# A decode attention block on one core: loop bodies of one group instead of two, a second buffer for the first chunk of transposed K, and the MLP's vector work behind the fourth tile

## The chip, the cores and the metric

The kernel runs on one core of one Trainium2 chip. TensorE (PE in the profile) multiplies matrices, with its weight loads shown as PEld; VectorE (DVE), ScalarE (ACT) and GpSimd (POOL) do the rest, and SyncE (SP) issues nearly all DMA transfers. The metric is the device time of one execution in microseconds (us). Lower is better.

## The reference

One token of a decoder block for two sequences (B = 2), with a cache of 32768 keys per head. Everything is float32.

```python
xn = _layernorm(x)                      # x: 2 x 1 x 512
q = (xn @ wq)                           # 32 query heads of 128
scores = q . k_cache * 128**-0.5        # 8 KV heads, 32768 keys, each serves 4 query heads
p = softmax(scores)
s = (p . v_cache) @ wo                  # 32 heads of 128 -> 512
gate, up = xn @ W_gate, xn @ W_up       # 512 -> 1792 each
g = silu((gate * (gate > 0) * up) @ W_down)
return x + s * g
```

K and V are 2 x 8 x 32768 x 128 floats each, 537 MB together. The weights come to 28 MB. All of it is read once.

## The kernel before

**Tiles and steps.** A group is one pair of sequence b and KV head hk. There are 16 groups (`NG`), and `group(g)` walks b fastest. A tile is 8192 keys of a group (`TK`): 4 MB of K and 4 MB of V. A group has four tiles (`NU`), so there are 64 (`NK`). The program goes in steps s = 0 to 68. Step s transposes K tile s and computes its scores; the softmax weights and V of tile s - 4 follow in the same step, so that a group's maximum is known before its weights are used.

**One step on the engines.** VectorE transposes the K tile in four chunks (`k_transpose(t, c)`, L645) from one of two K buffers (`kslot`) into one buffer per chunk (`kts[c]`). TensorE multiplies each chunk with the group's query (`scores`, L656): 16 matmuls of 512 columns, in four column strips. VectorE takes the scores of the tile before out of PSUM, with a running maximum (`take_scores`, L672). In each fourth step VectorE, TensorE and ScalarE form the group's maximum and the exponentials (`tile_maximum`, `maximum`), and the outcome of the group that is complete is scaled and turned (`take_o`, `finish_group`). TensorE brings the weights into their layout (`weights`), VectorE transposes them (`take_weights`), and in odd steps TensorE multiplies the weights of two tiles with V (`values`).

**Transfers.** V comes as 8 MB for two tiles (`load_vv`) into one buffer `wide`, which has no twin: the next pair can be asked for only when `values` has read the last one. SP takes its list in order and waits in front of each transfer until its buffer is free. The list begins: wq, K0, K1, W_gate and W_up, K2, K3, W_down, K4, K5, V0/1 (the first 8 MB of V), K6, K7, V2/3, and then two K and one V for each two steps. wq, W_gate, W_up, W_down all pass through `wide` before V does; V0/1 waits for the MLP's last product, which reads W_down there. K tile t + 2 waits for the fourth transposition of tile t.

**The MLP.** `mlp_gu` (step 1) multiplies with W_gate and W_up. `mlp_vector` (L590, five VectorE instructions) forms the hidden row, and `mlp_down` (L620, 56 matmuls of 128 columns) multiplies it with W_down. Both stand in the list `taken` of step 3: behind the first of tile 3's four transpositions and in front of `take_scores`.

**Waits and loops.** `Program.op` records every operation with the buffers that it reads and writes, and derives from them what each engine waits for. The order on each engine is that of the calls. `Program.emit` writes the list of each engine out; on VectorE and TensorE the steps from 8 to 63 become a loop whose body is `PERIOD` = 8 steps (two groups), seven rounds. Two groups are needed in a body because many buffers alternate by group (`st`, `mx`, `ls`, `os_`, `ops`, `qcur` and others have two sets), and because `finish_group` does its vector part only for the second sequence of a pair. TensorE's program holds 335 matmuls ahead of the loop, 272 in its body and 121 behind it, 728 in all.

**The first chunk.** `kts[0]` is one buffer, as are the other three: the first transposition of a tile waits until TensorE has read the first chunk of the tile before to the end.

Of the kernel before, what the change touches and what calls it, by code (L numbers as in the profile page):

```python
# [8 lines left out]
P = 128  # L9
Q = 32  # L10
# [6 lines left out]
PERIOD = 8  # L17
# [144 lines left out]
def decode_block_kernel(nc, x, kc, vc, wq, wo, wg, wu, wd, out):  # L162
# [14 lines left out]
    NST = 2 * NU  # L177
# [11 lines left out]
    kts = [sbuf(f"kts{c}", P, NR * P, align=ALIGN) for c in range(NC)]  # L189
    st = [sbuf(f"st{i}", P, NR * Q) for i in range(NST)]  # L190
# [16 lines left out]
    qcur = [sbuf(f"qcur{b}", P, 4, Q) for b in range(B)]  # L207
    ots = sbuf("ots", P, HKV, 4, 32)
    heads = sbuf("heads", P, B, REP, 32)
    fold = sbuf("fold", P, 32)  # L210
    stat = sbuf("stat", 32, 8)
    mx = [sbuf(f"mx{i}", P, NU) for i in range(2)]
    ls = [sbuf(f"ls{i}", P, NU) for i in range(2)]
    mcol = [sbuf(f"m{i}", P, 1) for i in range(2)]
    mr = [sbuf(f"mr{i}", 1, REP) for i in range(2)]
    nb = [sbuf(f"nb{i}", P, 1) for i in range(2)]
    lcol = [sbuf(f"l{i}", P, 1) for i in range(2)]
    rl = [sbuf(f"rl{i}", P, 1) for i in range(2)]
# [5 lines left out]
    ops = [bank(f"o{i}") for i in range(2)]  # L224
    ps_m = [bank(f"m_ps{i}") for i in range(2)]

# [69 lines left out]
    for i in range(2):  # L296
        dve(lambda e, i=i: e.memset(ops[i], 0.0), w=[f"o{i}"])
# [48 lines left out]
    for b in range(B):  # L346
        dve(lambda e, b=b: e.tensor_copy(heads[:, b, :, b], head), ["head"], ["heads"])
# [26 lines left out]
    xt = st[4].rearrange("p (r m) -> p r m", m=Q)  # L374
# [18 lines left out]
        ["st4"],  # L393
# [78 lines left out]
    def project_q():  # L472
        pq = ps_m
        for half in range(2):
            pe(
                chain(
                    [
                        mm(
                            pq[half][32 * c : 32 * c + 32, :],
                            xn[:, k, :],  # L480
                            wqt[:, k, half, c * 512 : (c + 1) * 512],
                            k == 0,
                            k == NKC - 1,
                        )
                        for k in range(NKC)
                        for c in range(4)
                    ]
                ),
                ["st4", "wide"],
                [f"m{half}"],  # L490
            )
# [52 lines left out]
        for g in range(2):  # L544
            take_query(g)

    def take_query(g):
        b, hk = group(g)
        pg.op(
            "POOL" if g >= 2 else "DVE",  # L550
            lambda e: e.tensor_copy(qcur[b], qt[:, b, hk]),
            ["qt"],
            [f"qcur{b}"],
        )
# [15 lines left out]
    def mlp_gu(which, i):  # L570
# [15 lines left out]
            ["st4", "wide", f"wide_{which}"],  # L586
# [3 lines left out]
    def mlp_vector():  # L590
        g, u = os_
        for i in range(2):
# [11 lines left out]
                st[NST - 1][:, : FI * Q], g[:, :FC].rearrange("p (f i) -> p i f", i=FI)  # L604
            ),
            ["os0"],
            [f"st{NST - 1}"],
# [12 lines left out]
    def mlp_down():  # L620
        ht = st[NST - 1][:, : FI * Q].rearrange("p (i m) -> p i m", m=Q)
        pe(
            chain(
                [
                    mm(
                        ps_m[0][32 * c : 32 * c + 32, :P],
                        ht[:, i, :],
                        wdt[:, i, c * P : (c + 1) * P],
                        i == 0,
                        i == FI - 1,  # L630
                    )
                    for i in range(FI)
                    for c in range(4)
                ]
            ),
            [f"st{NST - 1}", "wide"],
            ["m0"],
        )
        act(
            lambda e: e.activation(gy, ps_m[0][:, :P], AF.Silu, bias=zero, scale=1.0),  # L640
            ["m0", "zero"],
            ["gy"],
        )

    def k_transpose(t, c):  # L645
        src = kslot[t % 2]
        dve(
            lambda e: e.transpose(  # L648
                kts[c].rearrange("p (h n) -> p h n", h=2),
# [3 lines left out]
            [f"kts{c}"],  # L653
        )

    def scores(t):  # L656
        b, _ = group(t // NU)
        ps = ps_s[t % 2]

        def one(e, c):  # L660
            part = kts[c].rearrange("p (r e k) -> p r e k", e=4, k=Q)
            return mm(
                ps[Q * c : Q * c + Q, :], qcur[b][:, e, :], part[:, :, e, :], e == 0, e == 3
            )

        for c in range(NC):
            pe(one(0, c), [f"kts{c}", f"qcur{b}"], [f"s{t % 2}"])
        pe(chain([one(e, c) for e in (1, 2) for c in range(NC)]), [f"qcur{b}"], [f"s{t % 2}"])
        for c in range(NC):
            pe(one(3, c), [f"kts{c}", f"qcur{b}"], [f"s{t % 2}"])  # L670

    def take_scores(t):  # L672
        g, u = divmod(t, NU)
        dve(
            lambda e: e.tensor_scalar(  # L675
                st[t % NST],
# [5 lines left out]
                accum_out=mx[g % 2][:, u : u + 1],  # L682
            ),
            [f"s{t % 2}"],
            [f"st{t % NST}", f"mx{g % 2}_{u}"],
        )

    def tile_maximum(g):
        i = g % 2
        dve(  # L690
            lambda e: e.reduce_max(mcol[i], mx[i], axis=AX.X),  # L691
            [f"mx{i}_{u}" for u in range(NU)],
            [f"mcol{i}"],
        )
        pe(
            lambda e: e.transpose(ps_m[0][:1, :P], mcol[i], ident),  # L696
            [f"mcol{i}", "ident"],
            ["m0"],
        )

    def maximum(g):
        i = g % 2
# [3 lines left out]
                mr[i],  # L706
# [5 lines left out]
            [f"mr{i}"],  # L712
# [3 lines left out]
                mrow[:, :, :4, :], mr[i].unsqueeze(1).unsqueeze(1).to_broadcast([1, 4, 4, REP])  # L716
            ),
            [f"mr{i}"],
# [7 lines left out]
        dve(lambda e: e.tensor_copy(nb[i], pr[:, 256:257]), ["m0"], [f"nb{i}"])  # L726
        for u in range(NU):
            t = (g * NU + u) % NST
            act(
                lambda e, t=t, u=u: e.activation(  # L730
                    st[t], st[t], AF.Exp, bias=nb[i], scale=1.0, accum_out=ls[i][:, u : u + 1]
                ),
                [f"st{t}", f"nb{i}"],
                [f"st{t}", f"ls{i}_{u}"],
            )

    def weights(t):
        pe(
            mm(ps_p[t % 2], perm.rearrange("p k c h -> p (k c h)"), st[t % NST], True, True),
            ["perm", f"st{t % NST}"],  # L740
# [3 lines left out]
    def take_weights(t):  # L744
        dve(
            lambda e: e.transpose(st[t % NST], ps_p[t % 2]),  # L746
            [f"pt{t % 2}"],
            [f"st{t % NST}"],
        )

    def values(t):
        g, u = divmod(t, NU)
        at_, keys = place(t)
        w = st[t % NST].rearrange("p (r m) -> p r m", m=Q)

        def one(r):
            a = Q * (r % 4)
            moving = in_halves(at_)[:, r // 8, :, r % 8, :]
            return mm(
                ops[g % 2][a : a + NC * REP, :].rearrange("p (c d) -> p c d", c=NC),  # L760
                w[:, r, : NC * REP],
                moving,
# [4 lines left out]
        for h in range(2):  # L767
            held = keys if t < NK - 1 or h == 0 else ["wide1h"]
            pe(
                chain([one(r) for r in range(8 * h, 8 * h + 8)]),  # L770
                [f"st{t % NST}", *held],
                [f"o{g % 2}"],
            )

    def sums(g):
        i = g % 2
        dve(
            lambda e: e.reduce_sum(lcol[i], ls[i], axis=AX.X),
            [f"ls{i}_{u}" for u in range(NU)],
            [f"lcol{i}"],  # L780
        )
        pe(
            mm(ps_m[0][:, :1], same.rearrange("p r h -> p (r h)"), lcol[i], True, True),
            ["same", f"lcol{i}"],
# [3 lines left out]
    def take_o(g):  # L788
        i = g % 2
        dve(lambda e: e.reciprocal(rl[i], ps_m[0][:, :1]), ["m0"], [f"rl{i}"])  # L790
        dve(
            lambda e: e.scalar_tensor_tensor(  # L792
                os_[i].rearrange("p (c d) -> p c d", c=NC),
                ops[i].rearrange("p (c d) -> p c d", c=NC),
                rl[i],
# [4 lines left out]
            [f"o{i}", f"rl{i}", "own"],  # L800
            [f"os{i}"],
        )

    def finish_group(g):
        b, hk = group(g)
        pe(
            mm(
                ps_m[1],
                heads[:, b].rearrange("p h m -> p (h m)"),
                os_[g % 2],  # L810
                b == 0,
                b == B - 1,
            ),
            ["heads", f"os{g % 2}"],
            ["m1"],
        )
        if b < B - 1:
            return
# [9 lines left out]
        dve(  # L828
            lambda e: e.transpose(ot, ob),
            ["ob"],  # L830
            ["ot"],
        )
        act(
            lambda e: e.copy(ots[:, hk].rearrange("p j m -> p (j m)"), ot),
# [59 lines left out]
    extra, taken, ahead = {}, {}, {}  # L894
# [18 lines left out]
    at(taken, 3, mlp_vector)  # L913
    at(taken, 3, mlp_down)
# [6 lines left out]
    for s in range(END + 1):  # L921
        pg.step = s
        done = s // NU - 2 if s % NU == 0 and s >= 2 * NU else None
        full = s // NU - 1 if 0 < s <= NK and s % NU == 0 else None
# [3 lines left out]
        for f, a in taken.get(s, []):  # L928
            f(*a)
        if 0 < s <= NK:  # L930
            take_scores(s - 1)
        if done is not None:
            take_o(done)
        if full is not None:
            tile_maximum(full)
        if s < NK:
            k_transpose(s, 1)
        if full is not None:
            maximum(full)
# [11 lines left out]
        if s % NU == NU - 1 and s + NU + 1 < NK:  # L951
            take_query(s // NU + 2)
# [5 lines left out]
        if s % 2 and w > 0:  # L958
            for v in (w - 1, w):
                if v % NU == NU - 1:  # L960
                    sums(v // NU)
# [16 lines left out]
    with nc.Block(no_gpsimd_drain=True) as block:  # L978
# [54 lines left out]
```

## Time and profile before

| What | Value |
|---|---|
| median of 3 runs | 1315.36 us (1314.93 to 1316.49) |
| the profiled execution | 1317.09 us, of which the profile's span is 1315.2 us |
| PE, PEld, DVE busy | 903.2 us, 221.5 us, 695.4 us |
| HBM read | 564.67 MB, 429 GB/s over the span |
| mean granted TensorE clock | 0.83 |

The page of the profile has one row for each engine, a picture of the span in 40 slices, the DMA queues with the share of the 16 DMA engines' time that their packets took, the chain of work that ended last, and groups of instructions by line. The timeline gives single instructions with their start and duration. For a DMA issue the time is that of the issuing instruction, and the view of transfers gives the time from there to the landing. Queue q1 carries the data that SP asks for. The queue called "instruction" (q8) carries pieces of program that an engine fetches while it runs.

### The profile page before, as it was taken

How to read it: one execution, taken by the hardware profiler on the slowest of the kernel's cores; microseconds unless marked ns; L12 is line 12 of the kernel's file. 1: busy time of each engine (PE TensorE's matmuls, PEld its weight loads, DVE VectorE, ACT ScalarE, POOL GpSimd, SP SyncE). 2: the span in 40 equal slices, each digit the busy share in tenths (PEclk: the TensorE clock that was granted, in tenths of full speed). 3: DMA queues.
4: the chain of work that ended last, by engine and by line, in shares of the span. 5: the costliest groups of instructions: out<-in, count | busy, mean ns of one | idle time of the engine just before them, and what ended most of it. 6: DMA issues, size and time to landing. Idle time of an engine off the chain costs nothing.

```text
span 1315.2 us, 11033 instructions
## 1 busy us (share of the span) xinstructions
PE 903.2 (69%) x4700; PEld 221.5 (17%) x4700; DVE 695.4 (53%) x627; ACT 53.8 (4%) x141; POOL 4.8 (0%) x20
## 2 busy tenths in 40 slices
PE   3765767577676768667677766767767676786775
PEld 1121111111111112111111211111121111111111
DVE  3666645455654645665454666545466554546611
ACT  0000000000000000000000000000000000000000
POOL 0000000000000000000000000000000000000000
PEclk9788888897787788778788778878877888887798
DMA  9999999999999999999999999999999999999997
GB/s 408 434 417 430 433 443 419 442 428 430 432 438 441 435 424 432 434 438 441 431 433 426 438 434 438 435 433 436 427 432 433 439 440 431 426 433 433 439 431 318
DMA packets 16323, 564.89 MB, mean 429 GB/s; under 512 B 1826, under 2 KB 1842, under 8 KB 2228
## 3 DMA queue, kind: packets, MB, share of 16 engines
q1 hardware_dynamic: 16280, 564.67, 99.5%
q8 instruction: 11, 0.18, 0.0%
q14 instruction: 4, 0.03, 0.0%
q10 hardware_dynamic: 28, 0.01, 0.0%
HBM read 564.67 MB, written 0.00 MB: 429 GB/s over the span
## 4 chain that ended last, share of the span: by engine, by line
DMA 68%; DVE 19%; issue 7%; PE 5%; DVEq 0%; SPq 0%
DMA k<-in_A_k_cache_dram 61%; DVE kts L648 15%; DMA k<-in_A_wo_dram 3%; DMA w<-in_A_v_cache_dram 2%; DMA w<-in_A_wq_dram 2%; PE m_ps L240 2%; DVE st L675 2%; PE o L240 1%; PE s L240 1%; PE pt L240 1%; DVE ob L820 0%; DVE mrow L715 0%; DVE mr L705 0%; DVEq L150 0%; DVE m L691 0%
## 5 line engine op out<-in xcount | busy, mean ns | idle before, releaser
L648 DVE STREAM_TRANSPOSE kts<-k 128x2048 f32<-128x2048 f32 x256 | 578.2, 2291 | 524.5 <-DMA k<-in_A_k_cache_dram 427.6
L240 PE MATMUL s<-kts,qcur 128*32 128x512 f32 x2048 | 510.0, 734 | 215.9 <-DVE kts L648 215.7
L240 PE MATMUL o<-w,st 128*16 128x512 f32 x1984 | 236.7, 613 | 39.6 <-DMA w<-in_A_v_cache_dram 39.6
L240 PEld LDWEIGHTS s<-kts,qcur 128*32 128x32 f32 x2048 | 92.6, 128 | 636.0 <-DVE kts L648 462.3
L240 PEld LDWEIGHTS o<-w,st 128*16 128x16 f32 x1984 | 66.4, 99 | 188.1 <-issue 127.7
L730 ACT ACTIVATE st<-st,nb 128x512 f32<-128x512 f32 x64 | 45.4, 710 | 1121.7 <-DVE nb L726 1121.7
L240 PE MATMUL pt<-st,perm 128*128 128x512 f32 x128 | 83.4, 740 | 1.1 <-ACT st L730 1.1
L696 PE MATMUL m_ps<-ident,m 128*1 128x128 f32 x16 | 5.5, 347 | 84.8 <-DVE m L691 84.8
L746 DVE STREAM_TRANSPOSE st<-pt 128x512 f32<-128x512 f32 x64 | 43.3, 677 | 17.8 <-PE pt L240 17.7
L675 DVE TENSOR_SCALAR_CACHE_REDUCE st<-s 128x512 f32<-128x512 f32 x64 | 41.8, 653 | 3.1 <-PE s L240 3.1
L240 PEld LDWEIGHTS pt<-st,perm 128*128 128x128 f32 x128 | 23.9, 217 | 57.3 <-issue 45.4
L240 PE MATMUL m_ps<-negone,mrow 1*128 1x1 f32 x32 | 9.1, 351 | 33.2 <-DVE mrow L715 33.2
L240 PE MATMUL m_ps<-os,heads 128*128 128x512 f32 x32 | 31.3, 1079 | 0.0
L240 PE MATMUL m_ps<-w,st 128*32 128x128 f32 (+2 forms) x240 | 21.4, 514 | 13.0 <-DMA w<-in_A_wq_dram 8.0
L696 PEld LDWEIGHTS m_ps<-ident,m 128*1 128x1 f32 x16 | 1.3, 79 | 99.5 <-DVE m L691 99.5
L792 DVE SCALAR_TENSOR_TENSOR os<-o,rl,own 128x512 f32<-128x512 f32 x16 | 12.0, 751 | 9.4 <-PE o L240 8.4
L240 PEld LDWEIGHTS m_ps<-w,st 128*32 128x32 f32 x240 | 10.9, 137 | 22.8 <-issue 16.8
L240 PEld LDWEIGHTS m_ps<-negone,mrow 1*128 1x128 f32 x32 | 7.7, 298 | 37.5 <-DVE mrow L715 37.5
L790 DVE RECIPROCAL rl<-m_ps 128x1 f32<-128x1 f32 x16 | 2.6, 164 | 20.5 <-PE m_ps L240 20.5
L730 ACT ACTIVATION_READ_ACCUMULATOR st<-st,nb 128x1 f32 x64 | 11.9, 186 | 0.0
L381 PE MATMUL m_ps<-ident,st 32*128 32x32 f32 x4 | 0.7, 306 | 14.2 <-DVE st L370 14.2
L497 DVE COPY os<-m_ps 128x512 f32<-128x512 f32 x2 | 1.4, 692 | 16.2 <-PE m_ps L240 16.2
(75 smaller groups left out, 100.3 us busy)
## 6 DMA issues: line engine op xcount, KB each, us to landing
k<-in_A_k_cache_dram SPq DMA_DIRECT2D x64, 4096.0 KB, 26.1
k<-in_A_v_cache_dram SPq DMA_DIRECT2D x2, 4096.0 KB, 27.2
kts<-in_A_wo_dram SPq DMA_DIRECT2D x4, 1024.0 KB, 28.0
w<-in_A_v_cache_dram SPq DMA_DIRECT2D x1, 4096.0 KB, 33.6
w<-in_A_v_cache_dram SPq DMA_DIRECT2D x2, 2048.0 KB, 36.8
w<-in_B_W_gate_dram SPq DMA_DIRECT2D x1, 3584.0 KB, 19.6
w<-in_B_W_up_dram SPq DMA_DIRECT2D x1, 3584.0 KB, 27.7
w<-in_B_W_down_dram SPq DMA_DIRECT2D x1, 3584.0 KB, 17.8
```

Of the source, the lines that this page charges most:

```text
L240: return lambda e: e.matmul(out_, lhs, rhs, start=start, stop=stop, skip_group_check=True)
L381: lambda e, k=k: e.transpose(px[:, k * 32 : (k + 1) * 32], xquad[:, k, :], ident[:32, :32])
L497: dve(lambda e, q=qs, h=half: e.tensor_copy(q, pq[h]), [f"m{half}"], [f"os{half}"])
L648: lambda e: e.transpose(kts[c].rearrange("p (h n) -> p h n", h=2), in_halves(src)[:, :, c].rearrange("p h r d -> p h (r d)"),),
L675: lambda e: e.tensor_scalar(st[t % NST], ps_s[t % 2], SCALE, None, op0=ALU.mult, op1=ALU.max, accum_out=mx[g % 2][:, u : u + 1],),
L696: lambda e: e.transpose(ps_m[0][:1, :P], mcol[i], ident),
L730: lambda e, t=t, u=u: e.activation(st[t], st[t], AF.Exp, bias=nb[i], scale=1.0, accum_out=ls[i][:, u : u + 1]),
L746: lambda e: e.transpose(st[t % NST], ps_p[t % 2]),
L790: dve(lambda e: e.reciprocal(rl[i], ps_m[0][:, :1]), ["m0"], [f"rl{i}"])
L792: lambda e: e.scalar_tensor_tensor(os_[i].rearrange("p (c d) -> p c d", c=NC), ops[i].rearrange("p (c d) -> p c d", c=NC), rl[i], own.unsq ...
```

## The change

The loop body becomes one group (`PERIOD` = 4), and the loops begin at step 4: fifteen rounds. For that the buffers that alternated by group become single (`st` has four tiles instead of eight, with two buffers `wt` for the transposed weights; `mx`, `ls`, `mcol`, `mr`, `nb`, `lcol`, `rl`, `qcur`, the PSUM bank `o_ps`; group results use `os_[0]` alone), and each group does the same: `finish_group` runs its vector part for every group, 17 times instead of 8, and writes one column of `ots`. Step 4 has no finished group, so `take_o` and `finish_group` run there on zeros, with a first `total` of ones. The query of the next group is now copied by GpSimd at the end of each group, behind its last `scores`, where it was copied a group ahead. TensorE's program holds 163 matmuls ahead of the loop, 136 in the body and 121 behind it, 420 in all.

The first chunk of an odd tile is transposed into a fifth buffer, `kts[4]` (`turned`), so the first transposition of a tile no longer waits for the tile before.

`mlp_vector` and `mlp_down` move from behind the first transposition of tile 3 to the end of step 3, behind its fourth transposition and its `scores`. `mlp_down` now has 14 matmuls of 512 columns in four strips, a copy of the four partial sums out of a PSUM bank of its own (`ps_d`), and four matmuls that add the strips; it was 56 of 128 columns.

```diff
-PERIOD = 8
+PERIOD = 4
...
-    kts = [sbuf(f"kts{c}", P, NR * P, align=ALIGN) for c in range(NC)]
-    st = [sbuf(f"st{i}", P, NR * Q) for i in range(NST)]
+    kts = [sbuf(f"kts{c}", P, NR * P, align=ALIGN) for c in range(NC + 1)]
+    st = [sbuf(f"st{i}", P, NR * Q) for i in range(NU)]
+    wt = [sbuf(f"wt{i}", P, NR * Q) for i in range(2)]
...
-    qcur = [sbuf(f"qcur{b}", P, 4, Q) for b in range(B)]
+    qcur = sbuf("qcur", P, 4, Q)
...
-    ops = [bank(f"o{i}") for i in range(2)]
+    o_ps = bank("o")
     ps_m = [bank(f"m_ps{i}") for i in range(2)]
+    ps_d = bank("d")
...
     def take_query(g):
         b, hk = group(g)
-        pg.op(
-            "POOL" if g >= 2 else "DVE",
-            lambda e: e.tensor_copy(qcur[b], qt[:, b, hk]),
-            ["qt"],
-            [f"qcur{b}"],
-        )
+        pg.op("POOL", lambda e: e.tensor_copy(qcur, qt[:, b, hk]), ["qt"], ["qcur"])
...
     def mlp_down():
-        ht = st[NST - 1][:, : FI * Q].rearrange("p (i m) -> p i m", m=Q)
+        ht = wt[1][:, : FI * Q].rearrange("p (i m) -> p i m", m=Q)
         pe(
             chain(
                 [
                     mm(
-                        ps_m[0][32 * c : 32 * c + 32, :P],
+                        ps_d[32 * (i % 4) : 32 * (i % 4) + 32, :],
                         ht[:, i, :],
-                        wdt[:, i, c * P : (c + 1) * P],
-                        i == 0,
-                        i == FI - 1,
+                        wdt[:, i, :],
+                        i < 4,
+                        i >= FI - 4,
                     )
                     for i in range(FI)
...
+        dve(lambda e: e.tensor_copy(os_[0], ps_d), ["d"], ["os0"])
+        pe(
+            chain(
+                [
+                    mm(
+                        ps_d[32 * c : 32 * c + 32, :P],
+                        fold,
+                        os_[0][:, c * P : (c + 1) * P],
+                        True,
+                        True,
+                    )
                     for c in range(4)
...
+    def turned(t, c):
+        i = NC if c == 0 and t % 2 else c
+        return kts[i], f"kts{i}"
 
     def k_transpose(t, c):
         src = kslot[t % 2]
+        dst, key = turned(t, c)
         dve(
             lambda e: e.transpose(
-                kts[c].rearrange("p (h n) -> p h n", h=2),
+                dst.rearrange("p (h n) -> p h n", h=2),
                 in_halves(src)[:, :, c].rearrange("p h r d -> p h (r d)"),
             ),
             [f"k{t % 2}"],
-            [f"kts{c}"],
+            [key],
         )
...
     def finish_group(g):
-        b, hk = group(g)
+        b, hk = group(max(g, 0))
         pe(
-            mm(
-                ps_m[1],
-                heads[:, b].rearrange("p h m -> p (h m)"),
-                os_[g % 2],
-                b == 0,
-                b == B - 1,
-            ),
-            ["heads", f"os{g % 2}"],
+            mm(ps_m[1], heads.rearrange("p h m -> p (h m)"), os_[0], True, True),
+            ["heads", "os0"],
             ["m1"],
         )
-        if b < B - 1:
-            return
         dve(
...
         act(
-            lambda e: e.copy(ots[:, hk].rearrange("p j m -> p (j m)"), ot),
+            lambda e: e.copy(ots[:, hk, :, b], ot.rearrange("p (j m) -> p j m", j=4)[:, :, 0]),
             ["ot"],
             [f"ots{hk}"],
         )
...
-    at(taken, 3, mlp_vector)
-    at(taken, 3, mlp_down)
+    at(extra, 3, mlp_vector)
+    at(extra, 3, mlp_down)
+    at(extra, 3, total)
...
-        done = s // NU - 2 if s % NU == 0 and s >= 2 * NU else None
-        full = s // NU - 1 if 0 < s <= NK and s % NU == 0 else None
+        done = s // NU - 2 if s % NU == 0 and s >= NU else None
+        full = 0 < s <= NK and s % NU == 0
...
-        for f, a in taken.get(s, []):
-            f(*a)
...
-        if s % NU == NU - 1 and s + NU + 1 < NK:
-            take_query(s // NU + 2)
+        if s % NU == NU - 1 and s + 1 < NK:
+            take_query(s // NU + 1)
...
-            pg.emit("DVE", e, sems, loop=(PERIOD, NK))
+            pg.emit("DVE", e, sems, loop=(NU, NK))
...
-            pg.emit("PE", e, sems, loop=(PERIOD, NK))
+            pg.emit("PE", e, sems, loop=(NU, NK))
```

More of the change, by code (lines that the diff above doesn't have):

```diff
@@ L345, in decode_block_kernel @@
     )
-    for b in range(B):
-        dve(lambda e, b=b: e.tensor_copy(heads[:, b, :, b], head), ["head"], ["heads"])
+    dve(lambda e: e.tensor_copy(heads[:, :, 0], head), ["head"], ["heads"])
     dve(
@@ L652, in k_transpose @@
             [f"k{t % 2}"],
-            [f"kts{c}"],
+            [key],
         )
     def scores(t):
-        b, _ = group(t // NU)
         ps = ps_s[t % 2]
         def one(e, c):
[L661 to L664, printed above, removed]
+            part = turned(t, c)[0].rearrange("p (r e k) -> p r e k", e=4, k=Q)
+            return mm(ps[Q * c : Q * c + Q, :], qcur[:, e, :], part[:, :, e, :], e == 0, e == 3)
         for c in range(NC):
-            pe(one(0, c), [f"kts{c}", f"qcur{b}"], [f"s{t % 2}"])
-        pe(chain([one(e, c) for e in (1, 2) for c in range(NC)]), [f"qcur{b}"], [f"s{t % 2}"])
+            pe(one(0, c), [turned(t, c)[1], "qcur"], [f"s{t % 2}"])
+        pe(chain([one(e, c) for e in (1, 2) for c in range(NC)]), ["qcur"], [f"s{t % 2}"])
         for c in range(NC):
-            pe(one(3, c), [f"kts{c}", f"qcur{b}"], [f"s{t % 2}"])
+            pe(one(3, c), [turned(t, c)[1], "qcur"], [f"s{t % 2}"])
     def take_scores(t):
-        g, u = divmod(t, NU)
+        u = t % NU
         dve(
             lambda e: e.tensor_scalar(
-                st[t % NST],
+                st[u],
                 ps_s[t % 2],
@@ L768, in values, with total, sums, take_o @@
             held = keys if t < NK - 1 or h == 0 else ["wide1h"]
[L769 to L781, printed above, removed]
-        pe(
-            mm(ps_m[0][:, :1], same.rearrange("p r h -> p (r h)"), lcol[i], True, True),
-            ["same", f"lcol{i}"],
+            pe(chain([one(r) for r in range(8 * h, 8 * h + 8)]), [f"wt{t % 2}", *held], ["o"])
+    def total():
+        pe(
+            mm(ps_m[0][:, :1], same.rearrange("p r h -> p (r h)"), lcol, True, True),
+            ["same", "lcol"],
             ["m0"],
         )
-    def take_o(g):
-        i = g % 2
-        dve(lambda e: e.reciprocal(rl[i], ps_m[0][:, :1]), ["m0"], [f"rl{i}"])
+    def sums():
+        dve(lambda e: e.reduce_sum(lcol, ls, axis=AX.X), [f"ls{u}" for u in range(NU)], ["lcol"])
+        total()
+    def take_o():
+        dve(lambda e: e.reciprocal(rl, ps_m[0][:, :1]), ["m0"], ["rl"])
         dve(
             lambda e: e.scalar_tensor_tensor(
-                os_[i].rearrange("p (c d) -> p c d", c=NC),
-                ops[i].rearrange("p (c d) -> p c d", c=NC),
-                rl[i],
+                os_[0].rearrange("p (c d) -> p c d", c=NC),
+                o_ps.rearrange("p (c d) -> p c d", c=NC),
+                rl,
                 own.unsqueeze(2).to_broadcast([P, NC, DH]),
```

134 lines of the change are left out of this document (59 added, 75 removed).

## The prediction

> **What bounds the kernel now.** I read the page's busy times, queue rows and chain first.
>
> ```profile
> PE 903.2 (69%) x4700; PEld 221.5 (17%) x4700; DVE 695.4 (53%) x627; ACT 53.8 (4%) x141; POOL 4.8 (0%) x20
> DMA  9999999999999999999999999999999999999997
> q1 hardware_dynamic: 16280, 564.67, 99.5%
> q8 instruction: 11, 0.18, 0.0%
> DMA 68%; DVE 19%; issue 7%; PE 5%; DVEq 0%; SPq 0%
> ```
>
> The data queue keeps the 16 DMA engines busy for 99.5% of the span. TensorE (69%) and VectorE (53%) have room. So the change can only move the time by what it does to the stream of transfers. Next I looked at whether that stream ever falters, by pieces of the chain eight or sixteen tiles' transfers apart (start, duration, what), with the last transfer below them.
>
> ```profile
> 108.91 30.28 DMA k<-in_A_k_cache_dram
> 267.98 26.15 DMA k<-in_A_k_cache_dram
> 424.12 26.10 DMA k<-in_A_k_cache_dram
> 578.84 26.11 DMA k<-in_A_k_cache_dram
> 733.57 26.11 DMA k<-in_A_k_cache_dram
> 1272.42 37.65 DMA k<-in_A_wo_dram
> ```
>
> The landings are at 139.19, 294.13, 450.22, 604.95 and 759.68. Two groups thus take 154.9, 156.1, 154.7 and 154.7: it runs like clockwork, but one interval has 1.4 us too much. The last weights land at 1310.1, 5.1 before the span's end, and what follows is a fixed tail. The head is read from SP's timeline (issues; "x2" covers two, the second beginning 0.33 before the end) and the view of transfers, whose rows here are K3 (issued 59.68), W_down (70.18), K4 (79.41) and K5 (95.08), in this order, with the time to landing last.
>
> ```profile
> 46.46 13.55 SPq L237 DMA_DIRECT2D k<-in_A_k_cache_dram  x2
> 70.18 0.33 SPq L237 DMA_DIRECT2D w<-in_B_W_down_dram  x1
> 79.41 16.00 SPq L237 DMA_DIRECT2D k<-in_A_k_cache_dram  x2
> 95.45 0.43 SPq L237 DMA_DIRECT2D w<-in_A_v_cache_dram  x1
> k<-in_A_k_cache_dram SPq DMA_DIRECT2D x1, 4096.0 KB, 19.8
> w<-in_B_W_down_dram SPq DMA_DIRECT2D x1, 3584.0 KB, 17.8
> k<-in_A_k_cache_dram SPq DMA_DIRECT2D x1, 4096.0 KB, 18.3
> k<-in_A_k_cache_dram SPq DMA_DIRECT2D x1, 4096.0 KB, 15.1
> ```
>
> Landings: K3 79.5, W_down 88.0, K4 97.7, K5 110.2. K4 takes 9.7 behind its forerunner, K5 12.5: **2.8 us lost**. K5 was asked for only 2.6 before K4 landed; K4 was asked for 8.6 ahead and lost nothing. The queue ran dry at K5. Why it was late stands on VectorE and TensorE:
>
> ```profile
> 72.69 6.69 DVE L648 STREAM_TRANSPOSE kts<-k 128x2048 f32<-128x2048 f32 x3
> 79.44 3.62 PE L240 MATMUL s<-kts,qcur 128*32 128x512 f32 x26 [0.57 <-DVE kts L648]
> 82.35 2.31 DVE L648 STREAM_TRANSPOSE kts<-k 128x2048 f32<-128x2048 f32 x1 [2.97 <-PE s L240]
> 84.58 1.12 DVE L593 COPY os<-m_ps 128x448 f32<-128x448 f32 x2
> 87.79 0.65 DVE L675 TENSOR_SCALAR_CACHE_REDUCE st<-s 128x512 f32<-128x512 f32 x1
> 88.36 6.69 DVE L648 STREAM_TRANSPOSE kts<-k 128x2048 f32<-128x2048 f32 x3
> ```
>
> Tile 3's first transposition waits 2.97 for TensorE to leave the first chunk's buffer, and then the MLP (84.58 to 87.79, 3.2 us) stands between it and the other three. K5 goes out when those end, at 95.05.
>
> The other losses meet pieces of program. The first three rows are SP's issue of K0 and K1 and the time to landing of each; the others are queue rows of 38:41, 94:98, 130:303 and 306:310, and both instruction rows, data and code, of 326:1240, where q8 is missing.
>
> ```profile
> 1.19 0.89 SPq L237 DMA_DIRECT2D k<-in_A_k_cache_dram  x2
> k<-in_A_k_cache_dram SPq DMA_DIRECT2D x1, 4096.0 KB, 31.2
> k<-in_A_k_cache_dram SPq DMA_DIRECT2D x1, 4096.0 KB, 41.6
> q8 instruction: 1, 0.02, 2.0%
> q8 instruction: 1, 0.02, 1.4%
> q8 instruction: 5, 0.08, 0.2%
> q8 instruction: 1, 0.02, 1.5%
> q1 hardware_dynamic: 10218, 396.63, 100.3%
> q14 instruction: 2, 0.02, 0.0%
> ```
>
> K0 lands at 32.4 (the 31.2 row), K1 at 1.75 + 41.6 = 43.4: 11.0 instead of 9.7, 1.3 lost, with one piece in that time (2.0% of 16 engines' 3 us: 0.96 us of one engine). The 1.4 lost between 294 and 450 has the piece of 306:310 in it. But five pieces between 130 and 303 cost almost nothing (154.9 against 154.7). I read this so: a transfer has landed when the slowest of 16 engines is through; a piece that meets the engine that is last already costs 1.3 to 1.4, one that meets another costs nothing. All eleven come where code runs for the first time; while the loop repeats (326:1240) none does.
>
> **The change, part by part.** *K5 earlier.* With its own buffer, tile 3's first transposition starts when K3 has landed and VectorE is free (72.69 + 6.69 = 79.4): at 79.5, over at 81.8. `take_scores` needs TensorE's block to end, 79.44 + 3.62 = 83.1, and takes 0.65; the other three take 6.69. K5 goes out at about 90.4 instead of 95.1, 7.3 before K4 lands. Of the 2.8, I take all. Upper end 2.8; lower end 1.4, if the piece in 94:98 caused 1.4 of it and another takes its place. It is nearest to K4's row (8.6 ahead, no loss), so all.
>
> *The MLP behind tile 3.* Its 3.2 us now run at 90.4 to 93.6, after all that K5 waits for. TensorE's `scores` end at 94.0, then 14 matmuls, each two instructions in the trace: 28 at the 26 in 3.62 above, 3.9 us, to 97.9. SP's V0/1, next in its list, goes out then instead of at 95.45. K5 lands at 97.7 + 9.7 = 107.4, so V0/1 is 9.5 ahead, more than K4's 8.6: nothing. Behind it in the list stands K6, which waits for VectorE. VectorE waits for those matmuls, then copies (the like row above, 1.12 for two smaller ones: some 0.7) and is free at 98.6, 0.9 after K4 landed. If this cover fails (V0/1 after some 103), it costs what K5 cost, up to 2.8.
>
> *Step 4's empty group, and one vector part per group more.* From rows of the groups by line:
>
> ```profile
> L820 DVE TENSOR_REDUCE ob<-m_ps 128x128 f32<-128x512 f32 x8 | 5.3, 659 | 1.8 <-PE m_ps L240 1.8
> L829 DVE STREAM_TRANSPOSE ot<-ob 128x128 f32<-128x128 f32 x8 | 2.5, 312 | 0.3
> L792 DVE SCALAR_TENSOR_TENSOR os<-o,rl,own 128x512 f32<-128x512 f32 x16 | 12.0, 751 | 9.4 <-PE o L240 8.4
> L551 POOL COPY qcur<-qt 128x128 f32<-128x128 f32 x14 | 4.1, 293 | 1090.1 <-PE s L240 1090.1
> ```
>
> Step 4 gets 0.66 + 0.31 + 0.75 and small ones, about 2 us; K6, issued at 108.91 before, goes out at about 111.5. V0/1 lands near 126.8 (twice 9.7 behind K5), 15 later: nothing. Each second group gets 1.0 us on VectorE; the other half of the groups had it before, at the same interval. Nothing.
>
> *GpSimd's copy of the query* (0.29) now stands between the last `scores` of a group and the first of the next. TensorE's two tiles of `values` and a wait for K lie between. Nothing; without that cover 0.3 to 0.6 a group on TensorE, still hidden by the stream.
>
> *Less code.* 728 matmuls came in eleven pieces, 66 each; 420 need six or seven. The pieces up to 70 us stay (same code), so K1's 1.3 stays. The one near 308 goes: the loop's first round, steps 4 to 7, is over by about 178, when K8 lands (two tiles, 38.7, behind K6's 139.2). Gain 1.4 if no other piece meets the slowest engine twice, 0 if one does. With half as many, I take 1.4.
>
> *The tail.* The same transfers in the same order; the 5.1 stays.
>
> Sum: 2.8 + 1.4 = **4.2 us**. The profiled execution took 1317.09 with a span of 1315.2; the median of the runs is 1.7 below it. I take 4.2 from both: 1312.9 there, and 1315.36 - 4.2 = **1311.2** as the median, 0.32% faster. A measurement of this kernel can tell about 0.2%, 2.6 us, from no change.
>
> [...]
>
> **The rivals.** *Only one of the two gains* (2.8 or less: 1312.6 to 1314.0). K5 comes back but a piece still meets the slowest engine, or the pieces go and 7.3 ahead is not enough. For it: nothing in the page says which engine a piece meets; no issue in the head at 7.3 is there to compare.
>
> *Hidden anyway: no change*, 1315.4. The 2.8 could be another delay of one engine that moves to the next transfer. Against it: K5 is the only transfer with so short a lead, and the largest loss.
>
> *Slower: the short loop fetches its code each round.* Place: the jump back of TensorE, fourteen times. The body's 136 matmuls are two pieces; 28 pieces. If they meet eight engines in turn (the first and the ninth of the pieces, near 39 and 308, are the two that cost), the slowest gets 28/8 = 3.5 at 1.3: +4.6, and the 1.4 is not gained. With K5's 2.8 that is +1.8: 1317.2; it decides where the slowest engine gets more than two. Against it: the old body of 272 matmuls was jumped back to six times with no piece in 326:1240. [...]
>
> **How the numbers follow.** Both gains: 55%. One of the two: 27%, half of it with 2.6 or more. No change: 9%. Slower: 9%. So faster by over 0.2%: 0.55 + 0.13 = 0.68; within 0.2%: 0.14 + 0.09 = 0.23; slower 0.09. The range goes from 1309.8 (the sum and 1.4 more, should K1's piece also spare the slowest engine) to 1315.0, short of no change; the likeliest case alone has 1309.8 to 1312.4.
>
> **What would show it.** Right: K5 issued near 90.4, landing 9.7 behind K4; V0/1 issued near 98; six or seven q8 pieces, none after the first rounds until the tail; two groups in 154.7 throughout; data queue above 99.5%. Wrong: K5 still more than 10 behind K4; q8 pieces in mid-span; a V issued less than 3 before the K ahead of it lands, which would come from `values` held up by the query's copy or the single buffers.

## The result, and the profile after

| What | Before | After |
|---|---|---|
| median of 15 runs each | 1315.36 us (1314.3 to 1316.65) | 1312.69 us (1312.56 to 1313.45) |
| the profiled execution | 1317.09 us, span 1315.2 us | 1312.62 us, span 1310.8 us |

The ratio is 0.998 (95% interval 0.9972 to 0.9988): 2.7 us less, where 4.2 were forecast. The 15 runs after lie within 0.9 us of each other, those before within 2.4 us.

First the page after: span, busy times, the rows of two queues, and the chain's shares.

```profile
span 1310.8 us, 10865 instructions
PE 893.5 (68%) x4628; PEld 207.8 (16%) x4628; DVE 704.5 (54%) x646; ACT 54.7 (4%) x150; POOL 5.4 (0%) x22
q1 hardware_dynamic: 16280, 564.67, 99.7%
q8 instruction: 6, 0.10, 0.0%
DMA 71%; PE 13%; DVE 11%; issue 4%; SPq 0%; DVEq 0%
```

The bound is the same: 564.67 MB through one data queue, now busy for 99.7% of the span. Six pieces of program come in instead of eleven. Next is the chain after (start, duration, what), in pieces four tiles apart, with the last transfer below.

```profile
112.64 23.77 DMA k<-in_A_k_cache_dram
187.69 25.97 DMA k<-in_A_k_cache_dram
264.98 26.07 DMA k<-in_A_k_cache_dram
342.38 26.00 DMA k<-in_A_k_cache_dram
419.71 26.05 DMA k<-in_A_k_cache_dram
1267.93 37.67 DMA k<-in_A_wo_dram
```

The landings are at 136.41, 213.66, 291.05, 368.38 and 445.76: 77.3 a group, and two groups take 154.6 and 154.7. The interval that held 1.4 us too much is gone. K6 (the first row) lands 2.8 earlier than in the profile of before (139.19), and the last weights of the chain land at 1305.60, 5.2 ahead of the span's end. The tail is the same; the whole gain was made by the stream, 2.8 of the 4.5 between the two profiled executions before 137 us.

The head after, from SP's timeline (issues), with the time to landing of K4 (issued at 79.45), K5 (92.48) and V0/1 (99.39) below:

```profile
79.45 13.35 SPq L238 DMA_DIRECT2D k<-in_A_k_cache_dram  x2
99.39 0.33 SPq L238 DMA_DIRECT2D w<-in_A_v_cache_dram  x1
112.64 11.35 SPq L238 DMA_DIRECT2D k<-in_A_k_cache_dram  x2
k<-in_A_k_cache_dram SPq DMA_DIRECT2D x1, 4096.0 KB, 18.1
k<-in_A_k_cache_dram SPq DMA_DIRECT2D x1, 4096.0 KB, 14.8
w<-in_A_v_cache_dram SPq DMA_DIRECT2D x1, 27.2
```

K4 lands at 97.6, K5 at 107.3, V0/1 at 126.6. K5 is 9.7 behind K4, asked for 5.1 ahead of K4's landing, and nothing is lost. What lets it out stands on VectorE and TensorE:

```profile
72.73 9.06 DVE L664 STREAM_TRANSPOSE kts<-k 128x2048 f32<-128x2048 f32 x4
79.48 5.63 PE L241 MATMUL s<-kts,qcur 128*32 128x512 f32 x28 [0.28 <-DVE kts L664]
85.14 0.69 DVE L688 TENSOR_SCALAR_CACHE_REDUCE st<-s 128x512 f32<-128x512 f32 x1 [3.35 <-PE s L241]
85.76 6.70 DVE L664 STREAM_TRANSPOSE kts<-k 128x2048 f32<-128x2048 f32 x3
92.37 1.12 DVE L588 COPY os<-m_ps 128x448 f32<-128x448 f32 x2
99.40 0.69 DVE L633 COPY os<-d 128x512 f32<-128x512 f32 x1 [3.73 <-PE d L241]
```

Tile 3's first transposition now follows the last of tile 2 without a gap (72.73 + 9.06 covers four). The wait has become a shorter one in front of `take_scores`, 3.35 at 85.14, and the MLP begins at 92.37, when K5 is going out.

### The profile page after: what moved, and what is told of

Same layout as the page of the kernel before. It is cut to its first block, busy times and chain, and to the rows that moved or that the text cites. A ratio compares the mean times of both kernels' runs of the same rounds, so it can differ in the third digit from the quotient of the medians.

```text
span 1310.8 us, 10865 instructions
## 1 busy us (share of the span) xinstructions
PE 893.5 (68%) x4628; PEld 207.8 (16%) x4628; DVE 704.5 (54%) x646; ACT 54.7 (4%) x150; POOL 5.4 (0%) x22
## 3 DMA queue, kind: packets, MB, share of 16 engines
q1 hardware_dynamic: 16280, 564.67, 99.7%
HBM read 564.67 MB, written 0.00 MB: 431 GB/s over the span
## 4 chain that ended last, share of the span: by engine, by line
DMA 71%; PE 13%; DVE 11%; issue 4%; SPq 0%; DVEq 0%
DMA w<-in_A_v_cache_dram 35%; DMA k<-in_A_k_cache_dram 31%; PE o L241 10%; DVE kts L664 9%; DMA k<-in_A_wo_dram 3%; DMA w<-in_A_wq_dram 2%; PE s L241 2%; PE m_ps L241 1%; DVE st L688 1%; DVE ob L802 0%; PE pt L241 0%; SPq L238 0%; PE d L241 0%; DVE os L782 0%; DVE mrow L718 0%
## 5 line engine op out<-in xcount | busy, mean ns | idle before, releaser
L241 PE MATMUL s<-kts,qcur 128*32 128x512 f32 x2048 | 490.2, 708 | 204.8 <-DVE kts L664 204.8
L241 PE MATMUL o<-w,wt 128*16 128x512 f32 x1984 | 242.1, 636 | 73.4 <-DMA w<-in_A_v_cache_dram 73.3
L241 PEld LDWEIGHTS s<-kts,qcur 128*32 128x32 f32 x2048 | 88.2, 125 | 608.1 <-DVE kts L664 416.4
L241 PEld LDWEIGHTS o<-w,wt 128*16 128x16 f32 x1984 | 59.0, 101 | 238.6 <-issue 144.6
L703 PE MATMUL m_ps<-ident,mcol 128*1 128x128 f32 x16 | 5.4, 335 | 72.7 <-DVE mcol L702 72.7
L747 DVE STREAM_TRANSPOSE wt<-pt 128x512 f32<-128x512 f32 x64 | 43.3, 676 | 17.4 <-PE pt L241 17.2
L241 PE MATMUL m_ps<-w,wt 128*32 128x512 f32 (+1 forms) x128 | 15.5, 614 | 7.8 <-DMA w<-in_A_wq_dram 7.8
L802 DVE TENSOR_REDUCE ob<-m_ps 128x128 f32<-128x512 f32 x17 | 11.2, 659 | 2.8 <-PE m_ps L241 2.8
L732 ACT ACTIVATION_READ_ACCUMULATOR st<-st,nb 128x1 f32 x64 | 11.9, 186 | 0.0
L241 PE MATMUL o<-k,wt 128*16 128x512 f32 x64 | 9.0, 710 | 3.2 <-DMA k<-in_A_v_cache_dram 3.2
## 6 DMA issues: line engine op xcount, KB each, us to landing
w<-in_B_W_gate_dram SPq DMA_DIRECT2D x1, 3584.0 KB, 20.5
```

Source lines behind the costliest of these rows:

```text
L241: return lambda e: e.matmul(out_, lhs, rhs, start=start, stop=stop, skip_group_check=True)
L703: pe(lambda e: e.transpose(ps_m[0][:1, :P], mcol, ident), ["mcol", "ident"], ["m0"])
L732: lambda e, u=u: e.activation(st[u], st[u], AF.Exp, bias=nb, scale=1.0, accum_out=ls[:, u : u + 1]),
L747: dve(lambda e: e.transpose(wt[t % 2], ps_p[t % 2]), [f"pt{t % 2}"], [f"wt{t % 2}"])
L802: lambda e: e.reduce_sum(ob.rearrange("p (j q) -> p q j", j=4), ps_m[1].rearrange("p (c q j) -> p q j c", c=NC, j=4), axis=AX.X,),
```

## The experiments

Three explanations were on the table. *Lead*: the gain is K5's, and the shorter program is worth nothing. *Code*: the gain is the shorter program's, and K5's delay is made up or passed on later. *Halves*: each gives a part. A first run takes the profile of the kernel before once more, and two kernels do one part of the change each. The ratios are to the kernel before, run beside each experiment: its median was 1316.16 us beside the first four and 1315.73 us beside the last four.

**The kernel before, profiled again (b0).** No edit.

> The kernel before, unchanged, a second time: its median of 1315.4 us has to come again. The question is which span goes with it. The profiled execution of before had a span of 1315.2 and took 1317.09, above all its 15 runs; the profiled one of after had 1310.8 and took 1312.62, amid its runs. If the profile of before was simply a long execution, this one shows a span nearer 1313.5, the loss at K5 (landing 12.5 behind K4 instead of 9.7) is there again, and the losses near 43 and 308 us, which I gave to pieces of program, are smaller or elsewhere. If all three losses stand in every execution, the span is 1315 again.

Median 1315.29 us (1314.4 to 1316.29), ratio 0.9996 (0.9987 to 1.0005); the profiled execution took 1314.93. The page's span of it:

```profile
span 1313.1 us, 11033 instructions
```

SP's timeline, with the times to landing of the same K5 (issued at 95.92), V0/1 (96.29) and K6 (109.75) below:

```profile
95.92 0.33 SPq L237 DMA_DIRECT2D k<-in_A_k_cache_dram  x1
96.29 0.61 SPq L237 DMA_DIRECT2D w<-in_A_v_cache_dram  x1
109.75 0.33 SPq L237 DMA_DIRECT2D k<-in_A_k_cache_dram  x1
k<-in_A_k_cache_dram SPq DMA_DIRECT2D x1, 4096.0 KB, 12.1
w<-in_A_v_cache_dram SPq DMA_DIRECT2D x1, 31.1
k<-in_A_k_cache_dram SPq DMA_DIRECT2D x1, 4096.0 KB, 28.6
```

K5 goes out 0.8 later than in the profile of before, and yet it lands 2.2 earlier, at 108.0: 12.1 after its issue instead of 15.1. K4 had landed at 97.7, so K5 lost 0.6 here, not 2.8. V0/1 lands at 127.4, in step, and K6 at 138.3, 11.0 later where 9.7 would be in step: another 1.3, with a piece of program between 130 and 140. The piece near 308 is there as well, and the transfer around it (V, issued at 290.86, landed at 322.5) is only 19.5 behind the K ahead of it: no loss. The last weights stand in the chain as:

```profile
1270.24 37.66 DMA k<-in_A_wo_dram
```

They land at 1307.90, 2.3 later than after the change. So the execution profiled before was a long one, above all 82 timed runs of this kernel on record, and the 2.8 was a loss of that execution. The second one, at 1314.93, is on the short side of them.

**The head alone: long program, K5 early (b_head).** The kernel before, with the fifth buffer and with the MLP at the end of step 3; the loop keeps its eight steps and TensorE its 728 matmuls.

```diff
-    kts = [sbuf(f"kts{c}", P, NR * P, align=ALIGN) for c in range(NC)]
+    kts = [sbuf(f"kts{c}", P, NR * P, align=ALIGN) for c in range(NC + 1)]
...
+    def turned(t, c):
+        i = NC if c == 0 and t % 2 else c
+        return kts[i], f"kts{i}"
...
-    at(taken, 3, mlp_vector)
-    at(taken, 3, mlp_down)
+    at(extra, 3, mlp_vector)
+    at(extra, 3, mlp_down)
```

> Before, with the two edits of the head alone: the fifth buffer for the first chunk, and the MLP behind tile 3. Its loop stays at eight steps and its program at 728 matmuls. Theory lead (the whole gain is K5 asked for in time): 1312.7 us, as after, K5 issued near 92.5, landing 9.7 behind K4. Theory code (the gain is the pieces of program that are no longer fetched): 1315.4, no change. Both in halves: 1314.0.

Median 1314.10 us (1313.82 to 1314.33), ratio 0.9986 (0.9977 to 0.9995): part of the gain, 0.14% where the whole change has 0.20%. SP's timeline of it, then its time to landing of the V issued at 288.92, and the queue of program in 303:311:

```profile
79.73 13.18 SPq L237 DMA_DIRECT2D k<-in_A_k_cache_dram  x2
265.23 11.35 SPq L237 DMA_DIRECT2D k<-in_A_k_cache_dram  x2
288.92 0.33 SPq L237 DMA_DIRECT2D w<-in_A_v_cache_dram  x1
w<-in_A_v_cache_dram SPq DMA_DIRECT2D x1, 32.9
q8 instruction: 1, 0.02, 0.7%
```

K5 goes out at 92.58 and lands 9.6 behind K4, as after the change. But the V lands at 321.8, 20.8 behind the K that landed at 301.1, where 19.3 is in step: 1.5 lost with one piece of program in that time. This is the place and nearly the size that the prediction gave for the code, 1.4; 1314.10 - 1312.69 is 1.4 too.

**The short loop alone: K5 late (a_both).** The changed kernel with one buffer for the first chunk, and with the MLP, in its old product of 56 matmuls, back behind tile 3's first transposition.

```diff
-        i = NC if c == 0 and t % 2 else c
+        i = c
...
-    at(extra, 3, mlp_vector)
-    at(extra, 3, mlp_down)
+    at(taken, 3, mlp_vector)
+    at(taken, 3, mlp_down)
...
             k_transpose(s, 0)
+        for f, a in taken.get(s, []):
+            f(*a)
```

> After, with both edits of the head undone: one buffer for the first chunk, and the MLP, with its old product of 56 matmuls, behind tile 3's first transposition. The short loop stays. Theory lead: K5 is issued near 95 again, lands 12 behind K4, 1315.4 us. Theory code: 1312.7, as after, whatever K5 does. Both in halves: 1314.0.

Median 1315.11 us (1313.88 to 1315.48), ratio 0.9992 (0.9983 to 1.0001): no gain clear of the noise. Its K5 and V0/1 on SP's timeline and their times to landing, the chain's row of K6, and its queue of program in 120:130:

```profile
96.54 0.33 SPq L238 DMA_DIRECT2D k<-in_A_k_cache_dram  x1
k<-in_A_k_cache_dram SPq DMA_DIRECT2D x1, 4096.0 KB, 12.0
96.92 0.43 SPq L238 DMA_DIRECT2D w<-in_A_v_cache_dram  x1
w<-in_A_v_cache_dram SPq DMA_DIRECT2D x1, 31.0
112.05 26.85 DMA k<-in_A_k_cache_dram
q8 instruction: 1, 0.02, 0.6%
```

The queue of program in 120:130 in the changed kernel:

```profile
q8 instruction: 1, 0.02, 0.6%
```

K5 lands at 108.5, 10.7 behind K4 (97.8): 1.0 lost. V0/1 follows in step at 127.9, and K6 lands at 138.90, 11.0 behind it: another 1.3, with a piece in 120:130. After the change there is a piece in the same ten microseconds, and K6 lands 9.8 behind V0/1: it costs next to nothing there. 1.0 and 1.3 make 2.3; the medians differ by 2.4 (1315.11 against 1312.69).

With the two kernels themselves this makes a table of four, in medians:

| | K5 late | K5 early |
|---|---|---|
| long program | 1315.3 to 1316.2 | 1314.1 |
| short program | 1315.1 | 1312.7 |

The first cell is the kernel before, whose medians in four sets of runs were 1315.29, 1315.36, 1315.73 and 1316.16. So the early K5 is worth 2.4 with the short program and 1.2 to 2.1 with the long one, and the short program 1.4 with the early K5 and 0.2 to 1.1 with the late one. By the ratios the two parts make 0.14% and 0.08%, together 0.22%, against 0.20% for the whole. These times do not settle whether the parts add; what they share is seen in the packets further down.

**A long body (p12).** The changed kernel with a body of three groups: five rounds, 163 + 408 + 121 = 692 matmuls.

```diff
-PERIOD = 4
+PERIOD = 12
```

> After, with loop bodies of twelve steps instead of four (163 + 408 + 121 = 692 matmuls in TensorE's program instead of 420); every instruction that runs is the same, only more of them are written out. Theory lead: 1312.7, no change, though ten or so pieces of program are fetched instead of six. Theory code: 1.4 to 2.7 us longer, 1314 to 1315.4.

Median 1319.91 us (1319.71 to 1320.13), ratio 1.0032 (1.002 to 1.0044): 7.2 slower than with a body of one group, and more than any explanation gave. The two queues (packets, MB, share of 16 engines) in 326:1240 with this body:

```profile
q1 hardware_dynamic: 10185, 395.02, 100.1%
q8 instruction: 35, 0.57, 0.2%
```

The same stretch of the changed kernel, with a body of one group:

```profile
q1 hardware_dynamic: 10206, 396.60, 100.3%
q8 instruction: 1, 0.02, 0.0%
```

The body of 408 matmuls is fetched again in each round: 35 pieces in this stretch, 47 in all. K5 is in step here, 9.7 behind K4, and every transfer of K and V behind it is asked for at least 9.5 ahead. So 41 pieces more cost 7.2 us, 0.18 each on average, though each takes 0.9 to 1.0 of one DMA engine. From 250 us on, five landings some 195 us apart lose 1.3 to 1.6 each, 7.4 together; no other among the K and V tiles loses over 0.5. The prediction's reading (a piece costs 1.3 on its own engine, and pieces go round eight engines) makes 41/8 x 1.3 = 6.7 of it.

**One head edit at a time (a_mlp, a_kts).** The changed kernel with only the MLP put back (old place, old product), and with only the fifth buffer taken away. The edits are the two parts of the diff of the short loop alone.

> After, with only the MLP put back in its old place (behind tile 3's first transposition, with its old product of 56 matmuls); the fifth buffer stays. The first transposition then ends near 82, the MLP near 85, when TensorE's scores of the tile before are over as well, and three transpositions more give K5 at about 92.5, as in after. If the lead of K5 is what counts: no change, 1312.7 us. If the MLP's place itself counts: 1314 to 1315.

> After, with only the fifth buffer taken away. Tile 3's first transposition waits for TensorE to about 82.4, or 84.5 where its clock is low, and K5 goes out at 92.0 to 94.2. If the lead counts: 1312.7 us at 92, at most 0.5 more at 94. If the second buffer itself counts, in every odd tile: 1314 or more.

Both have a median of 1312.75 us (1312.64 to 1312.96, ratio 0.9976, 0.9967 to 0.9985; and 1312.65 to 1314.11, ratio 0.9978, 0.9969 to 0.9987), as the whole change. SP's timeline with only the MLP put back:

```profile
79.32 13.46 SPq L238 DMA_DIRECT2D k<-in_A_k_cache_dram  x2
92.82 0.43 SPq L238 DMA_DIRECT2D w<-in_A_v_cache_dram  x1
```

And with only the fifth buffer taken away:

```profile
92.74 0.33 SPq L238 DMA_DIRECT2D k<-in_A_k_cache_dram  x1
```

K5 goes out at 92.45 and 92.74, and lands 9.6 and 9.7 behind K4. Either edit brings K5 forward by about 4 us from 96.54; the second adds nothing, since K5 needs no more.

**K5 delayed by repeated work (d2, d4).** The changed kernel, in which tile 3's first transposition is done three and five times: 4.6 and 9.1 us more on VectorE ahead of K5 (2.28 each).

```diff
             k_transpose(s, 2)
+        if s == 3:
+            for _ in range(2):
+                k_transpose(s, 0)
```

The other has `range(4)`.

> After, with tile 3's first transposition done three times instead of once: K5 goes out 4.6 us later, near 97.1, a moment before K4 lands (97.6). In the runs so far with a late K5 it lands 12.0 us behind its issue (95.92 to 108.0, 96.54 to 108.5). If so: it lands at 109.1 instead of 107.3, 1.8 lost, and with all 16 engines level again the next piece of program costs 1.3 more: 1315.8 us. By the first profile of before (15.1 from issue to landing) it lands at 112.2: 4.9 lost, 1317.6. If the lead does not matter: 1312.7.

> The same with that transposition done five times: K5 goes out near 101.7, 4 us after the queue has run dry. With 12.0 from issue to landing: 113.7, 6.4 lost and 1.3 for the next piece, 1320.4 us. With 15.1: 116.8, 9.5 lost, 1322.2. If it is made up later: below 1317.

Medians 1314.83 us (1314.28 to 1316.46), ratio 0.9995 (0.9986 to 1.0004), and 1320.07 us (1319.24 to 1320.71), ratio 1.0032 (1.002 to 1.0044). K5's issue and time to landing with three transpositions, then K6's:

```profile
96.70 0.33 SPq L238 DMA_DIRECT2D k<-in_A_k_cache_dram  x1
k<-in_A_k_cache_dram SPq DMA_DIRECT2D x1, 4096.0 KB, 11.9
117.89 0.33 SPq L238 DMA_DIRECT2D k<-in_A_k_cache_dram  x1
k<-in_A_k_cache_dram SPq DMA_DIRECT2D x1, 4096.0 KB, 21.1
```

K5's with five:

```profile
100.35 0.33 SPq L238 DMA_DIRECT2D k<-in_A_k_cache_dram  x1
k<-in_A_k_cache_dram SPq DMA_DIRECT2D x1, 4096.0 KB, 12.1
```

The first lands at 108.6, 11.0 behind K4, and K6 at 139.0, 10.7 behind V0/1 (128.3): 1.3 and 1.0 lost. The second lands at 112.4, 14.9 behind K4: 5.2 lost, and V0/1 lands 20.5 behind it, 1.2 more. These make 2.3 and 6.4. The medians are 2.1 and 7.4 above the changed kernel's, but the executions in these two profiles took 1316.46 (the longest of its kernel's runs) and 1319.84, 3.8 and 7.2 above the profiled one of the changed kernel. So 1.5 of the first fell later (0.7 of it at V2/3, which lands 20.0 behind K7 where 19.3 is in step), and 0.8 of the second has no place in this account. The four late issues of the experiments, this one, 95.92, 96.54 and 96.70, land 11.9 to 12.1 after they go out. So in these runs K5 lands at the later of two times: K4's landing + 9.7, or its own issue + 12.0. By that a lead of 12.0 - 9.7 = 2.3 us is needed, and the runs with 4.8 to 7.2 show that more is worth nothing. The 2.3 is worked out and not measured: no run has a lead between 2.6 and 4.8, and the one with 2.6, the first profile of before, lost 2.8.

## Why the prediction was right or wrong

**Right in kind: what bounds the kernel.** The change moved the time only through the stream. TensorE's busy time fell by 10 us and VectorE's rose by 9, and neither shows in the time.

**K5 earlier: right mechanism, wrong size.** The step that failed is "I take 4.2 from both". Between the two profiled executions, 1317.09 and 1312.62, the gain was 4.5, close to the sum; between the medians it was 2.7. The 2.8 was what K5 lost in one execution, the longest of this kernel; the median execution did not have that much to give back. In the second profile K5 loses 0.6 at its landing, and K6 1.3 with the next piece of program. By the two profiles the gain of 2.3 (1307.90 against 1305.60 for the last weights) is 0.7 up to K5's landing, 1.2 from there to K6's, and 0.4 behind them. In the first profile K5 took 15.1 to land, where other late issues took 12.0, because of one DMA engine: the packets show 15 engines through with K5 within 0.9 of each other, and the one that had been last with K4 2.6 behind these. It had stood idle for 1.3, and its first packet of K5 took 2.7, where 1.2 is in step. Why it waited is open.

**The code: right size, a place that moves.** "The one near 308 goes: gain 1.4" holds with K5 early (1.5 at that V in the long program, 1.4 in the medians). But the kernel before has K5 late, and there the piece near 308 left no mark in the second profile; the piece at K6 did. Behind K4, in the kernel before, in the head alone, in the short loop alone and with K5 delayed, one piece costs 1.0 to 1.5. Its place is near 308 in the first profile of before and in the head alone, and at K6 or V0/1 in the other late ones. The two gains were read off one execution as if they were two separate defects, and were added.

**The reason, read from the packets.** The prediction read the rows so: a transfer has landed when the slowest engine is through, and a piece costs where it meets the engine that is last. The traces hold every packet, and each transfer ends on each of the 16 engines with a packet of 4 bytes. In the transfers of the table the last of these 16 falls 0.3 to 0.5 ahead of the landing. So the spread of the engines, from the first to the last, can be read at each landing (us):

| Profile | Spread at K4 | Spread at K5 | The piece | Spread ahead of it | Spread behind it | Landing late by |
|---|---|---|---|---|---|---|
| before, the first | 1.73 | 3.45 | 308.29, the ninth | 3.15 | 4.57 | 1.5 |
| before, the second | 1.62 | 0.58 | 131.63, the fourth | 0.56 | 1.68 | 1.3 |
| short loop alone | 1.88 | 0.52 | 128.60, the fourth | 0.51 | 1.67 | 1.3 |
| head alone | 2.04 | 2.04 | 305.54, the ninth | 2.04 | 3.46 | 1.5 |
| changed kernel | 1.71 | 1.71 | 126.10, the third | 1.71 | 1.82 | 0.2 |

While the stream is unbroken and no piece meets the last engine, the spread holds or narrows a little in these traces: in the changed kernel it is 1.82 at each landing from K6 to 1248 us, and in the first profile of before 4.57 at each from 324 to 1262 us, ahead of that 3.45 at K5 and 3.15 at 303 us. A piece sets the engine that it meets back by about 1.4: in the profiles of before (the first) and after, all 17 took 0.9 to 1.0 of their own, and the packet behind each took 0.5 longer. When the queue ran dry at K5 in the second profile of before and in the short loop alone, the engines came to rest nearly level (0.58 and 0.52), and the next piece made the engine that it met the last one. Without that, most pieces meet an engine that has room behind the last: in the first profile of before five pieces between 133 and 274 us left the spread no wider, 3.39 ahead of them and 3.15 behind. The pieces go round eight engines: with the long body, at 1236 us, eight engines are 6.4 to 8.1 behind the first and the other eight at most 2.2; in the first profile of before, at 324 us, seven are 1.0 to 1.6 and one 4.6 behind the first, and the other eight at most 0.3. So the ninth piece meets the engine of the first again, and that is the one near 308, in the head alone and in the first profile of before; there the engine that had waited at K5 was this one, and the others did not come level with it. The changed kernel has six pieces and no ninth.

**K5's time: off by 2.1, covered.** "K5 goes out at about 90.4" became 92.48, because TensorE's block of tile 2's scores took 5.63 instead of 3.62. The view of windows shows it for 79:86, here after. The columns behind the bounds and the length are the busy times of PE, PEld, DVE, ACT and POOL with their counts, then the granted clock, DMA's share and GB/s.

```profile
79.00:86.00 7.00, 5.83 (x29) 1.22 (x28) 3.60 (x5) 0.00 (x0) 0.00 (x0) 0.68 0.95 411
```

The same window before:

```profile
79.00:86.00 7.00, 3.62 (x26) 0.90 (x26) 4.03 (x5) 0.00 (x0) 0.00 (x0) 0.95 0.98 424
```

The clock granted in this window was 0.68 against 0.95. With the long body the same block took 3.68, and K5 went out at 90.54. That the change brought the lower clock isn't shown; a lead of 5.1 instead of 7.3 was still more than enough.

**What was costed at nothing stayed nothing.** V0/1 went out at 99.39 (forecast 97.9), VectorE was free at 100.1 (98.6), K6 went out at 112.64 (111.5): each 1.1 to 1.5 later than forecast. V0/1 was 7.9 ahead of K5's landing, K6 14.0 ahead of V0/1's. The groups' interval is 77.3 from the first to the fifth; step 4's empty group, the vector part in each group and GpSimd's copy of the query left no mark in it. The tail is 5.2 instead of 5.1.

**The pieces of program.** Six, as forecast at the lower end. "None after the first rounds until the tail" was wrong by one piece near 949 us, which cost nothing that the interval shows; what fetched it is open. K1's loss stayed: K0 landed at 32.2, K1 at 43.4.

**The rivals.** "Only one of the two gains" gave 1312.6 to 1314.0, and the time of 1312.69 lies in it, but the cause is another: K5 came back and no piece costs more than 0.2 between K5 and 446 us; there was less to win. The slower rival, code fetched in each round, is false for the body of 136 matmuls and true for one of 408: its place and its price were right. The runs put its beginning between 272 and 408 matmuls: in 326:1240 no piece came in with the body of 272 (the kernel before), and 35 came with that of 408. By the prediction's 66 matmuls a piece the body of 272 is four pieces and that of 408 is six; the latter took seven in its first pass and nine in each later round, and whether all of these are TensorE's the trace doesn't say. To the data stream the 41 pieces cost 7.2 us.

## What to carry to other kernels

In a kernel bound by one stream of transfers, look for the transfer whose lead over the end of the one ahead is shorter than what an idle queue needs from issue to landing beyond the steady interval (here 12.0 - 9.7 = 2.3 us at least, and 4.8 was enough); beyond that, an earlier issue buys nothing, and one of two edits that each reach it is enough. Size a gain of a few microseconds from more than one profiled execution, and treat losses that meet at the same resource as one account: here the delay levelled the DMA engines, and that decided which piece of program would cost something, so their prices could not be read off apart. Keep a loop's body short enough not to be fetched again in each round (here 272 matmuls were short enough, 408 weren't), since such code takes time from the data even where every transfer is asked for in time: here 7.2 us for 41 pieces.

## What the runs showed that was not expected

The same piece of program, in the same 10 us of the same transfer, costs 1.3 us when the queue ran dry some 20 us earlier and at most 0.2 when it didn't: what counts is how far behind the others the engine is that it meets. A body of 408 matmuls (12 steps) is fetched anew in every round and makes the kernel 7.2 us slower, where one of 272 isn't fetched again at all. And with the late K5 gone, the spread of the runs narrowed from 2.4 to 0.9 us. The kernels with a late K5 have spreads of 1.5 to 2.4, those with an early one 0.3 to 0.9, one single run apart. The two profiles of the kernel before show why that can be: the same late K5 lost 2.8 in one execution and 0.6 in the other.
